# Pinning the conversion of weights and the forming of sums in a fused attention and two-MLP kernel

## The chip, the cores and the metric

The kernel runs on one core of a Trainium2 chip. The metric is the device time of one execution in microseconds (us). The core has five engines that run side by side, each working through its own instructions in order: TensorE (PE, matrix products; its weight loads are shown as PEld), VectorE (DVE), ScalarE (ACT), GpSimd (POOL) and SyncE (SP). Here POOL and SP mainly issue DMA transfers, each from its own queue.

## The reference

Linear attention feeds a first MLP, and that feeds a second one.

```python
q_s = softmax of q over the head's 64 columns          # q, k, v: 4 x 8 x 576 x 64
k_s = softmax of k over the 576 tokens
x = q_s @ (k_s.T @ v)                                  # as 2304 tokens x 512

h = x @ w_in                                           # first MLP: 512 -> 2048
g = s * relu(h) ** 2 + b
x = g @ w_out                                          # 2048 -> 512

h = x @ w_in2                                          # second MLP: 512 -> 2048
g = h * tanh(log1p(exp(min(h, 20))))                   # mish (h itself above 20 in the softplus)
out = g @ w_out2                                       # 2048 -> 512
```

The weights arrive as 64-bit floats. The kernel has to turn their bits into 32-bit floats itself.

## The kernel before, in words

**Three passes.** Most products are made of split operands. A tile t of 32-bit floats is cast on ACT to a high half (line 175), and DVE subtracts that from t to get the low half (line 172). PE then runs three fast passes: high by high, high by low, low by high (`passes`, line 178).

**First MLP.** The 2304 tokens run in five chunks of 512, 256, 512, 512 and 512. For every chunk there are 16 slots, one for each 128 columns of the hidden layer; slot n makes h of step n + 2 (`emit_h`), squares it, and adds step n into the four output banks (`emit_y`). There are 80 slots. Attention for chunk c + 1 is done in seven stages (`att1` to `att5_mm`) for four groups of two heads, spread over the slots of chunk c: for chunk 1, group hp begins in slot 2 hp + 3, with `att2` one slot later, `att3` two, `att4` three and `att5` four slots later.

**The weights of the first MLP** are made during chunk 0, in 16 pairs j, each of 128 x 1024 elements: one block of w_in (j + 1) and one of w_out (j - 1). A pair is loaded (`load_w`), then `conv_bits` takes its magnitude on ACT (line 129) and runs four DVE instructions that put the 32-bit value together in a tile t (lines 130 to 141), and `conv_split` casts and subtracts it to the halves w. Step f of the first nine h (and the first seven y) of chunk 0 uses t as it is, in slow full-precision products (lines 220 and 263); the pairs 0 to 7 are therefore split only in slots 12 to 19, the pairs 8 to 15 in slots 6 to 13. A pair j from 8 on is needed by h in slot j - 1; pair 1 and those after it are needed by chunk 1 from slot 15 + j on.

**Second MLP.** It uses a scheme of seven products (P1 to P7) for a 2 x 2 block product, instead of eight. Its inputs are sums and differences of blocks. The weights' sums are made all along the first MLP, in 32 units (`unit_sums`, `unit_split`), and stored in DRAM. Chunks are taken in pairs, (0, 2) and then (3, 4); chunk 1 comes last and in plain form. For a pair, `b_load` brings the first MLP's output back from DRAM into a tile with four spots, and `b_steps` makes the sums one product after the other, in place: `diff3`, `sum2`, `diff41`, and after each the split of one operand. The sums of pair (0, 2) are made in the last 14 slots (`put_slot`). Those of pair (3, 4) are made while pair (0, 2) is worked on: the first half goes out to DRAM (`put_dram`), the second is made later and joined with it (`put_both`). `h_unit` makes the seven products of eight such units F and adds them up into four spots of g (DVE, line 460), with mish on ACT. `y_pair` then makes the seven products of g with w_out2, splitting one spot of each g for each product (gly_P, ghy_P), and changes the spots in place between the products: in `y_pair`, too, `diff41` computes two differences in one DVE instruction of 128 x 1024. Three tiles each (tags gh and gl) hold the halves of g; `put_dram` takes its two tiles from the same three.

Weights of the second MLP come back from DRAM through a ring of tiles (`ring_load`, on the POOL queue).

**Order.** The program is traced in one order, and a planner then orders each engine's instructions by times that it works out itself. An instruction may so be put ahead of ones that were traced before it, as soon as the planner takes its inputs as ready. `pin` (`keep_in_program_order`) forbids this for one instruction: it stays behind the instruction traced just before it on the same engine. Later ones that are not pinned may still go ahead of it.

```python
        run(n, "att5", "att2", "att3", "early")
        if n < NF:
            run(n, "split", "bits")
...
        run(n, "bits", "split", "unit")
        run(n, "keep", "load")
```

These lines of the main loop fix the order inside slot n; between them lie h, the activation, the rest of attention and y.

Of the kernel before, what the change touches and what calls it, by code (L numbers as in the profile page):

```python
# [31 lines left out]
def kernel(  # L32
# [67 lines left out]

    w_raw, w_t, W = {}, {}, {}

# [21 lines left out]

    def bits(t, raw, pin=lambda ins: None):

        high, low = raw[..., 1], raw[..., 0]
        ti = t.bitcast(I32)
        pin(nc.scalar.activation(out=t, in_=high.bitcast(F32), func=AF.Abs))
# [15 lines left out]

    def conv_bits(j):
# [9 lines left out]
        raw = w_raw.pop(j)  # L156
        if j:
            bits(t, raw, pin if j > 4 else lambda ins: None)
        else:
            for i in range(2):  # L160
                bits(t[:, i], raw[:, i])

    def conv_split(j):

        home = j if j >= WHOLE else j - 1
        w = wp.tile([P, 2, 2, DM], F32R, tag=f"w{home}" if home >= 0 else "last", name=f"w{j}")
        split(w[:, :, 0], w[:, :, 1], w_t.pop(j))
        for i, (z, f) in enumerate(members(j)):
            W[z, f] = (w[:, i, 0], w[:, i, 1])
# [123 lines left out]

    def pin(ins):
        tc.keep_in_program_order(ins)

    def unit_load(e):
# [12 lines left out]
    def unit_sums(e):  # L310

        u = cv.tile([P, 8, P], F32, tag="t1", name=f"u{e}")
        u_t[e] = u
        bits(u[:, 3:7].rearrange("p b d -> p (b d)"), u_raw.pop(e), pin)
        if e + 1 < len(units):
# [30 lines left out]
    def diff3(t):  # L346
        nc.vector.tensor_tensor(out=t[:, 3], in0=t[:, 2], in1=t[:, 3], op=ALU.subtract)

    def sum2(t):
        nc.vector.tensor_tensor(out=t[:, 0], in0=t[:, 3], in1=t[:, 0], op=ALU.add)  # L350

    def diff41(t):
        nc.vector.tensor_tensor(  # L353
            out=t.rearrange("p (a b) n -> p b a n", b=2)[:, 1], in0=t[:, 1:3],
            in1=t[:, 0:1].to_broadcast([P, 2, CM]), op=ALU.subtract,
        )

    def b_steps(pair, kb, put):

        t = b_raw.pop(kb)  # L360
        if pair == 0:
            for spot in range(2):
                b = bsum[:, 2 * spot + kb:2 * spot + kb + 1]
                nc.vector.tensor_scalar(out=t[:, spot], in0=t[:, spot], scalar1=b, scalar2=None, op0=ALU.add)
        for r in Y_ORDER:
            if r == "P7":
                diff3(t)
            elif r == "P6":
                sum2(t)
            elif r == "P5":  # L370
                diff41(t)
            put(r, kb, t[:, SPOT[r]])
            yield
# [5 lines left out]
    def put_slot(r, kb, src):  # L379
        if kb == 0:  # L380
            x_op[r] = wp.tile([P, 2, 2, CM], F32R, tag=f"w{Y_ORDER.index(r)}", name=f"xo{r}")
        split(x_op[r][:, 0, kb], x_op[r][:, 1, kb], src, pin=pin)

    def put_dram(r, kb, src):
        hi, lo = g_tiles(f"b{r}_{kb}", CM)
        split(hi, lo, src)
        for i, t in enumerate((hi, lo)):
            nc.sync.dma_start(out=x_dram[r][:, i], in_=t.bitcast(F32))

    def put_both(r, kb, src):  # L390
        x_op[r] = wp.tile([P, 2, 2, CM], F32R, tag=f"w{Y_ORDER.index(r)}", name=f"xo{r}")
        pin(nc.gpsimd.dma_start(out=x_op[r][:, :, 1 - kb], in_=x_dram[r]))
        split(x_op[r][:, 0, kb], x_op[r][:, 1, kb], src)

# [47 lines left out]
    def h_unit(pair, F):  # L442
# [45 lines left out]
        ring_load()  # L488

    def y_pair(pair, more):  # L490

# [19 lines left out]
        for r in Y_ORDER:  # L511
            p[r] = ps = bank(r)
            for F in range(NU):
# [9 lines left out]
                if r == "P7" and F % 2:  # L523
                    sum2(g_all[NU // 2 + F // 2])
                if r == "P2" and F % 2:
                    diff41(g_all[F // 2])
                if r == "P6" and F % 2:
                    diff41(g_all[NU // 2 + F // 2])
                if F % 4 == 3:
# [364 lines left out]
    for j in range(NF):  # L894
        at(j - 5 if j > 4 else -3 if j < 3 else -2, "load", load_w, j)
        at(max(j - 3, -1) if j else -2, "bits", conv_bits, j)
        at(j - 2 if j >= WHOLE else NF - 4 + j, "split", conv_split, j)
    L0 = (NC - 1) * NF
# [11 lines left out]
    for kb in range(2):  # L910
        at(L0 + 2 * kb, "load", b_load, 0, kb, f"ws{kb}")
        for i in range(7):
            at(L0 + 2 + 5 * kb + i, "unit", b_next, kb)
    for s in (6, 10, 14):
        at(L0 + s, "load", ring_load)
# [33 lines left out]
    for n in range(NS):  # L949
# [7 lines left out]
        if n < NF:  # L957
            run(n, "split", "bits")
        run(n, "att4_mm")
# [14 lines left out]
        if f == NF - 1:  # L974
            y_out(c)
        run(n, "bits", "split", "unit")
        run(n, "keep", "load")
# [93 lines left out]
```

## Time and profile before

| | |
|---|---|
| time, median of 3 runs | 855.45 us (854.0 to 856.22) |
| the profiled execution: its own time, and its span | 859.47 us, 857.7 us |
| PE busy | 827.5 us, 96% of the span |
| PEld busy | 665.4 us, 78% |
| DVE busy | 615.4 us, 72% |
| ACT busy | 439.8 us, 51% |
| POOL busy | 109.1 us, 13% |
| granted TensorE clock, mean | 0.993 |

The span runs from the first to the last instruction of the profiled execution. PE's busy time is modelled and its products overlap, so the share says that PE is rarely without work, not that it runs at its best. A clock of 1.0 stands for 2.4 GHz, 0.5 for 1.2 GHz.

### The profile page before, as it was taken

How to read it: one execution, taken by the hardware profiler on the slowest of the kernel's cores; microseconds unless marked ns; L12 is line 12 of the kernel's file. 1: busy time of each engine (PE TensorE's matmuls, PEld its weight loads, DVE VectorE, ACT ScalarE, POOL GpSimd, SP SyncE). 2: the span in 40 equal slices, each digit the busy share in tenths (PEclk: the TensorE clock that was granted, in tenths of full speed). 3: DMA queues.
4: the chain of work that ended last, by engine and by line, in shares of the span. 5: the costliest groups of instructions: out<-in, count | busy, mean ns of one | idle time of the engine just before them, and what ended most of it. 6: DMA issues, size and time to landing. Idle time of an engine off the chain costs nothing.

```text
span 857.7 us, 11568 instructions
## 1 busy us (share of the span) xinstructions
PE 827.5 (96%) x4084; PEld 665.4 (78%) x4084; DVE 615.4 (72%) x1157; ACT 439.8 (51%) x787; POOL 109.1 (13%) x192
## 2 busy tenths in 40 slices
PE   4899998999999999999999999989999999999998
PEld 2444786999888888888887888778788888878897
DVE  7789897678877788877678567787764755786411
ACT  3645667557655656565565544355442333544421
POOL 4000000000000101121112211001111111112110
PEclk9999999999999999999999999999999999999999
DMA  7983422254556666467658699657678866688891
GB/s 188 313 306 113 127 77 70 68 154 131 184 188 197 212 220 217 163 207 250 206 172 255 197 362 333 192 176 237 214 247 265 235 198 204 220 295 261 259 378 59
DMA packets 90473, 179.01 MB, mean 209 GB/s; under 512 B 26928, under 2 KB 45104, under 8 KB 86832
## 3 DMA queue, kind: packets, MB, share of 16 engines
q0 software_dynamic: 30256, 112.73, 40.4%
q1 hardware_dynamic: 59072, 64.50, 24.4%
q10 hardware_dynamic: 1088, 1.05, 0.4%
q8 instruction: 32, 0.52, 0.2%
q14 instruction: 25, 0.20, 0.1%
HBM read 131.60 MB, written 46.66 MB: 208 GB/s over the span
## 4 chain that ended last, share of the span: by engine, by line
PE 57%; issue 23%; DMA 7%; DVE 6%; POOL 3%; SPq 2%; ACT 1%; POOLq 0%; DVEq 0%
PE P L182 19%; PE h L182 8%; PE y L182 8%; PE h L220 3%; PE y L263 3%; PE rh L182 3%; PE ry L182 3%; DMA xdP<-glbP 2%; POOL wdo L331 2%; DVE g L353 2%; DMA b<-yd 2%; POOL wdi L331 2%; PE P1y L182 1%; DVE gly_P L172 1%; PE P3y L182 1%
## 5 line engine op out<-in xcount | busy, mean ns | idle before, releaser
L182 PE MATMUL h<-xh,w 128*128 128x512 f32 (+1 forms) x568 | 177.2, 375 | 1.2 <-ACT xh L175 0.7
L182 PE MATMUL y<-gh,w 128*128 128x512 f32 (+1 forms) x584 | 176.2, 368 | 0.0
L182 PE MATMUL P<-xoP,rw 128*128 128x512 f32 x672 | 156.4, 390 | 3.2 <-DVE s L460 1.7
L182 PEld LDWEIGHTS P<-xoP,rw 128*128 128x128 f32 x672 | 125.4, 188 | 30.6 <-DVE s L460 3.1
L182 PEld LDWEIGHTS h<-xh,w 128*128 128x128 f32 x568 | 105.1, 192 | 19.5 <-ACT r L245 1.4
L182 PEld LDWEIGHTS y<-gh,w 128*128 128x128 f32 x584 | 106.3, 188 | 17.8
L175 ACT CAST ghy_P<-g 128x512 fp32r<-128x512 f32 x112 | 69.7, 623 | 82.5 <-DVE gly_P L172 34.6
L182 PE MATMUL y<-gl,w 128*128 128x512 f32 (+1 forms) x292 | 106.8, 367 | 0.0
L172 DVE TENSOR_TENSOR gly_P<-g,ghy_P 128x512 fp32r<-128x512 f32 x112 | 76.0, 688 | 41.4 <-ACT ghy_P L175 39.5
L182 PE MATMUL h<-xl,w 128*128 128x512 f32 (+1 forms) x284 | 105.1, 371 | 0.0
L460 DVE TENSOR_TENSOR s<-s,P 128x512 f32<-128x512 f32 x112 | 75.2, 685 | 39.9 <-PE P L182 28.9
L182 PE MATMUL P<-ghy_P,rw 128*128 128x512 f32 x224 | 87.5, 392 | 0.0
L463 ACT ACTIVATE g<-s 128x512 f32<-128x512 f32 x64 | 39.5, 631 | 76.8 <-DVE s L460 76.4
L175 ACT CAST umem<-u 128x512 fp32r<-128x512 f32 x64 | 37.3, 619 | 55.5 <-DVE u L318 54.2
L182 PEld LDWEIGHTS y<-gl,w 128*128 128x128 f32 x292 | 55.0, 188 | 9.0
L182 PEld LDWEIGHTS h<-xl,w 128*128 128x128 f32 x284 | 54.5, 192 | 8.9 <-DVE xl L172 0.3
L245 ACT ACTIVATE r<-h 128x512 f32<-128x512 f32 (+1 forms) x80 | 43.9, 552 | 31.0 <-PE h L182 20.7
L172 DVE TENSOR_TENSOR gl<-r,gh 128x512 fp32r<-128x512 f32 (+1 forms) x73 | 45.9, 629 | 18.6 <-ACT gh L175 18.2
L172 DVE TENSOR_TENSOR umem<-u,umem 128x512 fp32r<-128x512 f32 x64 | 42.3, 685 | 9.8 <-ACT umem L175 9.5
L182 PEld LDWEIGHTS P<-ghy_P,rw 128*128 128x128 f32 x224 | 42.2, 189 | 8.2
L248 ACT ACTIVATE r<-r 128x512 f32<-128x512 f32 (+1 forms) x80 | 46.8, 589 | 1.7
L182 PE MATMUL P<-gly_P,rw 128*128 128x512 f32 x112 | 45.1, 403 | 1.3 <-DVE gly_P L172 0.9
(185 smaller groups left out, 1300.7 us busy)
## 6 DMA issues: line engine op xcount, KB each, us to landing
rw<-wdo POOLq DMA_DIRECT2D x28, 1024.0 KB, 5.1
wdi<-umem POOLq DMA_DIRECT2D x32, 512.0 KB, 3.7
wdo<-umem POOLq DMA_DIRECT2D x32, 512.0 KB, 3.9
rw<-wdi POOLq DMA_DIRECT2D x16, 1024.0 KB, 7.1
rw<-wdi POOLq DMA_DIRECT2D x16, 768.0 KB, 6.6
raw<-in_moe_w_in_dram SPq DMA_DIRECT2D x16, 512.0 KB, 7.1
raw<-in_moe_w_out_dram SPq DMA_DIRECT2D x16, 512.0 KB, 9.3
ur<-in_moe_w_in_dram SPq DMA_DIRECT2D x16, 512.0 KB, 4.3
```

The lines of the kernel that those rows point to most:

```text
L172: pin(eng.tensor_tensor(out=lo, in0=src, in1=hi.bitcast(F32), op=ALU.subtract))
L175: pin(nc.scalar.copy(out=hi, in_=src))
L182: mm = nc.tensor.matmul(out=ps, lhsT=x, rhs=y, start=start, stop=stop)
L220: nc.tensor.matmul(out=h_ps[m], lhsT=wl[:, o], rhs=x_whole[kk], start=kk == 0, stop=kk == NK - 1,)
L245: op = nc.scalar.activation(out=r, in_=h_ps.pop(m), func=AF.Relu)
L248: nc.scalar.activation(out=r, in_=r, func=AF.Square)
L263: nc.tensor.matmul(out=ps, lhsT=wl[:, o], rhs=gl, start=f == 0, stop=False)
L331: nc.gpsimd.dma_start(out=to.rearrange("p b h d -> p b (h d)"), in_=u_mem[0][:, half].rearrange("p b h d -> p b (h d)"),)
L353: nc.vector.tensor_tensor(out=t.rearrange("p (a b) n -> p b a n", b=2)[:, 1], in0=t[:, 1:3], in1=t[:, 0:1].to_broadcast([P, 2, CM]), op=AL ...
L460: nc.vector.tensor_tensor(out=out, in0=a, in1=b, op=ALU.add)
L463: nc.scalar.activation(out=g[:, spot], in_=src, func=AF.Mish)
```

## The change

- The first MLP's weights are made in four events, each with its own place. `conv_size` (the magnitude on ACT) and `conv_bits` (DVE) come in slot j - 3. `conv_high` (the cast on ACT) comes at the end of slot j - 3 for the pairs from 8 on, and at the end of slot 12 + j for the first eight. `conv_low` (the subtraction on DVE) comes at the start of the slot after that, behind attention's `att5`, `att2` and `att3` of that slot. The casts and the subtractions are pinned; the magnitude stays pinned from pair 5 on. Pairs from 6 on are loaded one slot earlier, and pair 5 before the first slot.
- All sums of the second MLP's x, and their splits on both engines, are pinned (`b_steps`, `put_slot`, `put_dram`, `put_both`).
- `diff41` is gone. Each of its two differences is a DVE instruction of its own (`less0`): in `b_steps` one before P5 and one before P4, in `y_pair` at places written out in two lists (`TO3`, `TO1`) over P2, P6, P5 and P4.
- The first three ring loads move from slots 6, 10 and 14 of the last chunk to its slots 2, 9 and 14.

The arithmetic and the number of bytes moved stay the same.

```diff
-    def bits(t, raw, pin=lambda ins: None):
+    def size(t, raw, pin=lambda ins: None):
+        pin(nc.scalar.activation(out=t, in_=raw[..., 1].bitcast(F32), func=AF.Abs))
+
+    def bits(t, raw):
...
-    def conv_split(j):
+    def conv_high(j):
 
         home = j if j >= WHOLE else j - 1
         w = wp.tile([P, 2, 2, DM], F32R, tag=f"w{home}" if home >= 0 else "last", name=f"w{j}")
-        split(w[:, :, 0], w[:, :, 1], w_t.pop(j))
+        pin(nc.scalar.copy(out=w[:, :, 0], in_=w_t[j]))
+        w_new[j] = w
+
+    def conv_low(j):
+
+        w = w_new.pop(j)
+        minus(nc.vector, w[:, :, 1], w_t.pop(j), w[:, :, 0], pin)
...
-    def diff41(t):
-        nc.vector.tensor_tensor(
-            out=t.rearrange("p (a b) n -> p b a n", b=2)[:, 1], in0=t[:, 1:3],
-            in1=t[:, 0:1].to_broadcast([P, 2, CM]), op=ALU.subtract,
-        )
+    def less0(t, out, src):
+        return nc.vector.tensor_tensor(out=t[:, out], in0=t[:, src], in1=t[:, 0], op=ALU.subtract)
...
         for r in Y_ORDER:
             if r == "P7":
-                diff3(t)
+                pin(diff3(t))
             elif r == "P6":
-                sum2(t)
+                pin(sum2(t))
             elif r == "P5":
-                diff41(t)
+                pin(less0(t, 3, 2))
+            elif r == "P4":
+                pin(less0(t, 1, 1))
...
-        split(x_op[r][:, 0, kb], x_op[r][:, 1, kb], src, pin=pin)
+        split(x_op[r][:, 0, kb], x_op[r][:, 1, kb], src, pin, pin)
...
+    TO3 = tuple(("P2", F) for F in (1, 3, 4, 5, 7)) + tuple(("P6", F) for F in (1, 3, 5))
+    TO1 = tuple(("P5", F) for F in (1, 3, 5)) + tuple(("P4", F) for F in range(5))
...
-                if r == "P2" and F % 2:
-                    diff41(g_all[F // 2])
-                if r == "P6" and F % 2:
-                    diff41(g_all[NU // 2 + F // 2])
+                if (r, F) in TO3:
+                    less0(g_all[TO3.index((r, F))], 3, 2)
+                if (r, F) in TO1:
+                    less0(g_all[TO1.index((r, F))], 1, 1)
...
-        at(j - 5 if j > 4 else -3 if j < 3 else -2, "load", load_w, j)
+        at(j - 6 if j > 5 else -3 if j < 3 else -2, "load", load_w, j)
+        if j > 4:
+            at(j - 3, "early", conv_size, j, pin)
+        else:
+            at(max(j - 3, -1) if j else -2, "bits", conv_size, j)
         at(max(j - 3, -1) if j else -2, "bits", conv_bits, j)
-        at(j - 2 if j >= WHOLE else NF - 4 + j, "split", conv_split, j)
+        s = j - 3 if j >= WHOLE else NF - 4 + j
+        at(s, "keep", conv_high, j)
+        at(s + 1, "early", conv_low, j)
...
-    for s in (6, 10, 14):
+    for s in (2, 9, 14):
         at(L0 + s, "load", ring_load)
```

## Rows read from the trace of the kernel before

**Rows 1.** The page: busy time of the engines and share of the span.
```profile
PE 827.5 (96%) x4084; PEld 665.4 (78%) x4084; DVE 615.4 (72%) x1157; ACT 439.8 (51%) x787; POOL 109.1 (13%) x192
```

**Rows 2.** PE's waits: engine, line, releaser: us in total, times, longest us.
```profile
PE P1y L182 <- DVE s L460: 2.5, 1, 2.5
PE x L182 <- ACT qth L827: 2.0, 1, 2.0
...
PE P L182 <- DVE s L460: 1.7, 1, 1.7
PE P L182 <- DMA rw<-wdi: 1.5, 2, 1.2
```

**Rows 3.** Windows: stretch, its length, busy time of each engine, clock, DMA share.
```profile
142.00:148.70 6.70, 2.93 (x17) 2.01 (x15) 3.91 (x8) 5.14 (x10) 0.00 (x0) 0.86 0.33 120
148.70:153.60 4.90, 4.90 (x22) 4.85 (x23) 4.83 (x10) 4.51 (x12) 0.20 (x2) 0.50 0.23 72
456.80:458.50 1.70, 0.50 (x3) 0.11 (x2) 0.81 (x2) 1.64 (x4) 1.20 (x2) 1.00 1.07 400
...
536.40:538.70 2.30, 0.62 (x4) 0.20 (x2) 2.30 (x5) 0.04 (x1) 0.00 (x0) 1.00 0.99 301
566.60:569.40 2.80, 0.28 (x3) 0.02 (x1) 2.80 (x5) 2.23 (x5) 0.00 (x0) 1.00 0.87 322
569.40:573.50 4.10, 4.10 (x11) 3.24 (x12) 4.10 (x7) 3.22 (x6) 0.00 (x0) 0.58 0.03 12
600.00:608.00 8.00, 7.36 (x30) 5.11 (x29) 7.54 (x11) 2.86 (x5) 1.23 (x2) 1.00 0.69 231
758.00:766.00 8.00, 7.34 (x30) 5.10 (x29) 7.55 (x11) 2.85 (x5) 1.28 (x2) 1.00 0.71 234
...
597.00:608.00 11.00, 10.36 (x43) 7.52 (x42) 10.54 (x14) 4.26 (x8) 1.58 (x3) 1.00 0.70 227
608.00:619.00 11.00, 11.00 (x51) 9.07 (x50) 7.65 (x12) 4.85 (x9) 1.78 (x3) 1.00 0.64 207
```

**Rows 4.** The chain of work around 144: start, us, engine and line.
```profile
143.56 0.95 ACT w L175
...
144.53 1.23 DVE w L172
145.76 0.34 DVE qtl L172
```

**Rows 5.** DVE and POOL in order of time: start, us, what [idle before, releaser].
```profile
451.22 0.71 POOL L418 DMA_DIRECT2D rw<-wdi  x1
...
536.13 0.69 DVE L172 TENSOR_TENSOR gly_P<-g,ghy_P 128x512 fp32r<-128x512 f32 x1 [0.78 <-DMA xdP<-glbP]
...
562.53 0.69 DVE L347 TENSOR_TENSOR b<-b 128x512 f32<-128x512 f32 x1 [2.14 <-DMA b<-yd]
```

**Rows 6.** Groups by line: shapes and count, busy us, mean ns, idle before.
```profile
L172 DVE TENSOR_TENSOR w<-t,w 128x1024 fp32r<-128x1024 f32 x16 | 19.6, 1223 | 5.1 <-ACT w L175 5.1
...
L353 DVE TENSOR_TENSOR g<-g 128x1024 f32<-128x1024 f32 x16 | 19.3, 1217 | 0.1
...
L347 DVE TENSOR_TENSOR g<-g 128x512 f32<-128x512 f32 x16 | 11.0, 686 | 3.8 <-ACT g L463 3.8
```

**Rows 7.** Chunk 0: two of attention's DVE steps, in order of time.
```profile
99.91 0.42 DVE L764 TENSOR_TENSOR qn<-q,qs 128x256 f32<-128x256 f32 x1
...
137.47 0.42 DVE L764 TENSOR_TENSOR qn<-q,qs 128x256 f32<-128x256 f32 x1
```

**Rows 8.** The chain of work: the first h products of slots 8 and 12.
```profile
95.36 1.13 PE h L182 x5
...
120.57 1.81 PE h L182 x8
```

**Rows 9.** DMA issues: queue, count, KB each, median us from issue to landing.
```profile
yd<-ys SPq DMA_DIRECT2D x16, 256.0 KB, 2.8
...
xdP<-glbP SPq DMA_DIRECT2D x7, 256.0 KB, 9.5
```

More of the change, by code (lines that the diff above doesn't have):

```diff
@@ L98, in segments, with pin @@
         return found
-    w_raw, w_t, W = {}, {}, {}
+    def pin(ins):
+        tc.keep_in_program_order(ins)
+    w_raw, w_t, w_new, W = {}, {}, {}, {}
     def members(j):
@@ L123, in load_w @@
         w_raw[j] = raw.rearrange("p z (n w) -> p z n w", w=2)
-    def bits(t, raw, pin=lambda ins: None):
+    def size(t, raw, pin=lambda ins: None):
+        pin(nc.scalar.activation(out=t, in_=raw[..., 1].bitcast(F32), func=AF.Abs))
+    def bits(t, raw):
         high, low = raw[..., 1], raw[..., 0]
         ti = t.bitcast(I32)
-        pin(nc.scalar.activation(out=t, in_=high.bitcast(F32), func=AF.Abs))
         nc.vector.tensor_scalar(
@@ L144, in bits, with conv_size @@
         )
-    def conv_bits(j):
+    def conv_size(j, pin=lambda ins: None):
         if j < WHOLE:
@@ L155, in conv_bits @@
             W[z, f] = (None, t[:, i])
-        raw = w_raw.pop(j)
         if j:
-            bits(t, raw, pin if j > 4 else lambda ins: None)
+            size(t, w_raw[j], pin)
+    def conv_bits(j):
+        t, raw = w_t[j], w_raw.pop(j)
+        if j:
+            bits(t, raw)
         else:
             for i in range(2):
+                size(t[:, i], raw[:, i])
                 bits(t[:, i], raw[:, i])
-    def conv_split(j):
+    def conv_high(j):
         home = j if j >= WHOLE else j - 1
         w = wp.tile([P, 2, 2, DM], F32R, tag=f"w{home}" if home >= 0 else "last", name=f"w{j}")
-        split(w[:, :, 0], w[:, :, 1], w_t.pop(j))
+        pin(nc.scalar.copy(out=w[:, :, 0], in_=w_t[j]))
[3 more added lines that the diff above has]
+        minus(nc.vector, w[:, :, 1], w_t.pop(j), w[:, :, 0], pin)
         for i, (z, f) in enumerate(members(j)):
@@ L292 @@
     u_mem, u_raw, u_t = [], {}, {}
-    def pin(ins):
-        tc.keep_in_program_order(ins)
     def unit_load(e):
@@ L313, in unit_sums @@
         u_t[e] = u
-        bits(u[:, 3:7].rearrange("p b d -> p (b d)"), u_raw.pop(e), pin)
+        raw = u_raw.pop(e)
+        size(u[:, 3:7].rearrange("p b d -> p (b d)"), raw, pin)
+        bits(u[:, 3:7].rearrange("p b d -> p (b d)"), raw)
         if e + 1 < len(units):
@@ L346, in diff3 @@
     def diff3(t):
-        nc.vector.tensor_tensor(out=t[:, 3], in0=t[:, 2], in1=t[:, 3], op=ALU.subtract)
+        return nc.vector.tensor_tensor(out=t[:, 3], in0=t[:, 2], in1=t[:, 3], op=ALU.subtract)
     def sum2(t):
-        nc.vector.tensor_tensor(out=t[:, 0], in0=t[:, 3], in1=t[:, 0], op=ALU.add)
-    def diff41(t):
-        nc.vector.tensor_tensor(
-            out=t.rearrange("p (a b) n -> p b a n", b=2)[:, 1], in0=t[:, 1:3],
-            in1=t[:, 0:1].to_broadcast([P, 2, CM]), op=ALU.subtract,
-        )
+        return nc.vector.tensor_tensor(out=t[:, 0], in0=t[:, 3], in1=t[:, 0], op=ALU.add)
+    def less0(t, out, src):
+        return nc.vector.tensor_tensor(out=t[:, out], in0=t[:, src], in1=t[:, 0], op=ALU.subtract)
     def b_steps(pair, kb, put):
@@ L363, in b_steps @@
                 b = bsum[:, 2 * spot + kb:2 * spot + kb + 1]
-                nc.vector.tensor_scalar(out=t[:, spot], in0=t[:, spot], scalar1=b, scalar2=None, op0=ALU.add)
+                pin(nc.vector.tensor_scalar(out=t[:, spot], in0=t[:, spot], scalar1=b, scalar2=None, op0=ALU.add))
         for r in Y_ORDER:
             if r == "P7":
-                diff3(t)
+                pin(diff3(t))
             elif r == "P6":
-                sum2(t)
+                pin(sum2(t))
             elif r == "P5":
-                diff41(t)
+                pin(less0(t, 3, 2))
+            elif r == "P4":
+                pin(less0(t, 1, 1))
             put(r, kb, t[:, SPOT[r]])
@@ L381, in put_slot @@
             x_op[r] = wp.tile([P, 2, 2, CM], F32R, tag=f"w{Y_ORDER.index(r)}", name=f"xo{r}")
-        split(x_op[r][:, 0, kb], x_op[r][:, 1, kb], src, pin=pin)
+        split(x_op[r][:, 0, kb], x_op[r][:, 1, kb], src, pin, pin)
     def put_dram(r, kb, src):
         hi, lo = g_tiles(f"b{r}_{kb}", CM)
-        split(hi, lo, src)
+        split(hi, lo, src, pin, pin)
         for i, t in enumerate((hi, lo)):
@@ L392, in put_both @@
         pin(nc.gpsimd.dma_start(out=x_op[r][:, :, 1 - kb], in_=x_dram[r]))
-        split(x_op[r][:, 0, kb], x_op[r][:, 1, kb], src)
+        split(x_op[r][:, 0, kb], x_op[r][:, 1, kb], src, pin, pin)
     ring, ring_at = [], [0, 0]
@@ L957 @@
         if n < NF:
-            run(n, "split", "bits")
+            run(n, "bits")
         run(n, "att4_mm")
@@ L975 @@
             y_out(c)
-        run(n, "bits", "split", "unit")
+        run(n, "unit")
         run(n, "keep", "load")
```

## The prediction

> **What bounds the kernel now.** I read the page first: PE is busy for 96% of the span, DVE for 72% [rows 1]. So the end is set by PE, and a change that removes no product can only win where PE stands still or runs at half clock, and can only lose by adding such places. The next view is PE's own list of waits [rows 2]. It is short. Setting aside the start, which the change leaves as it is, the long ones are for DVE's sums of the second MLP's products (line 460: 2.5 and 1.7 us), for a high half in attention (2.0 us) and for a ring load (1.2 us at its longest). The third view, windows cut around these places [rows 3], prices them. PE's idle time is the length of a window less its busy time:
>
> - 142.0 to 148.7 (chunk 0 turns into chunk 1): 6.70 - 2.93 = 3.8 us idle. The clock falls behind it. At 0.86 over 6.7 us, 28% or 1.9 us of the window run at 1.2 GHz instead of 2.4, then 4.9 us at 0.50. Half of that time is lost, 3.4 us. Together 7.2 us.
> - 456.8 to 458.5: 1.2 us, the ring load.
> - 536.4 to 538.7: 1.7 us, behind line 460.
> - 566.6 to 569.4: 2.5 us, behind line 460, and then a clock of 0.58 over 4.1 us, so 3.4 us at 1.2 GHz, 1.7 us lost. Together 4.2 us.
> - 600 to 608 and 758 to 766: 0.6 and 0.7 us, in the products with w_out2 of either pair. DVE is busy there for 10.54 of 11 us, against 7.65 in the next 11 us.
>
> That is 15.6 us in six places; the half clock came only behind the two longest stops. All six lie where the change works. Sums go against the profiled execution, 859.47 us; I take them off the median of 855.45 us unscaled, since both are the same program 4 us apart.
>
> **The first MLP's weights.** Removed: nothing. The 16 casts and 16 subtractions stay, 1.22 us of DVE each [rows 6]. What changes is that they can't float any more. At 142 us PE waits for the x of attention's last group, and the chain of work to that x runs through a weight's cast (0.95 us) and a weight's subtraction (1.23 us), and only then comes attention's own subtraction qtl [rows 4]. The half being made there belongs to pair 5 (counted along the 16), which the code places in slot 17; PE is at the end of slot 15. With the pins, pair 5's cast is at the end of slot 17, behind the activation traced there, so those two steps leave the chain: 0.95 + 1.23 = 2.2 us. What remains of the 3.8 us is 1.6 us, shorter than the 1.7 us at 536.4, behind which the next window shown still has a clock of 1.00 [rows 3]. So I also count the 3.4 us of half clock as won: 5.6 us. Bounds: nothing (other work fills the chain) and all 7.2 us. I take 5.6, the steps seen in the chain.
>
> The price is that a low half now stands behind attention. In slots 7, 9 and 11 `conv_low` is pinned behind `att3`, whose last DVE step is qn, and qn needs the buffer that PE's x of the group before must first release. For group 1 (groups counted from 0) qn ended at 99.91 + 0.42 = 100.33 us; a low half behind it ends at 101.6. But slot 8's h, which reads it, started at 95.36 [rows 7, 8]: 6.2 us late. For group 3 it is 137.89 + 1.23 = 139.1 against 120.57: 18.5 us late. Below, the price is nothing: qn was itself held up by the floating halves and bits in front of it, PE can take attention's small products ahead of h, and DVE's four steps of `bits`, not pinned, can fill the wait. I charge one qn and one low half once, 0.4 + 1.2 = 1.65 us, near the lower end, since a pair's nominal slot still lies a whole slot ahead of its use. Queued behind a waiting low half are the next pair's bits and then the activation's low halves; two steps of h ahead cover those.
>
> The magnitude was pinned before, from pair 5 on, and moves within its slot. The loads one slot earlier concern SyncE's queue alone, and by the code's order their tiles are free then: nothing on the path. In chunk 1 the splits of pairs 3 to 7 no longer run ahead, so some 5 x 1.2 = 6 us of DVE work moves behind 150 us, two slots ahead of its use: no charge, covered by DVE's idle time there; if that cover is gone, each costs PE at most its 1.2 us.
>
> **The ring loads.** The first load was issued at 451.22 [rows 5], pinned on POOL's queue behind a weight store of its slot, and PE waited for it 1.2 us. Four slots earlier takes it past the stores of two or three units on that queue; its tile ("last") is free since the last chunk began. It then lands well ahead of PE: 1.2 us won, lower bound nothing. The second and third loads shift by one slot and none, and no wait of PE names them.
>
> **The pinned sums.** At 562.53 DVE had stood for 2.14 us at `diff3` of the second half of pair (3, 4), waiting for b to land [rows 5]. This step is needed only for the pair after. Behind it in DVE's order stood the sums of line 460 that PE waited for until 569.4. Pinned, the step is behind the P7 products' low halves, tens of us after the load. The stop and its half clock go: 4.2 us, lower bound nothing (see the rivals). At 536.13 DVE stood 0.78 us, for the second time in a row, at a low half of g for `y_pair`, whose tile was still being written out by `put_dram` [rows 5]; the sums that PE wanted came after it. With the x sums pinned in units 2 to 6 the three tiles are taken later, and such a low half can't be put ahead of all of them any more: 1.7 us, lower bound nothing. The seven splits that move into `y_pair` add a step of some 0.69 us to each product of about 11 us, where DVE has 3.3 us free outside P2 [rows 3].
>
> **The differences apart.** One 128 x 1024 step took 1.217 us, two of 128 x 512 take 2 x 0.686 = 1.372 us [rows 6]: 0.155 us more, 20 times, 3.1 us of DVE work in all. In exchange eight double steps that all fell into P2 become 16 single ones over four products. The saturated stretch loses three of its eight double steps' worth, 8 x 1.217 - 5 x 0.686 = 6.3 us of DVE time, and three other products get 2.1 to 3.4 us, which about fills the 3.3 us that DVE had free from 608 to 619. The two stops go: 0.64 + 0.66 = 1.3 us, lower bound nothing.
>
> The Trainium skill (VectorE: DVE Perf Modes, section on the TRN2 errata) speaks against this edit: each DVE instruction on SBUF pays a fixed latency, a large tile once and small ones each time. The rows agree with it by the 0.155 us per split; by that rule, the edit costs DVE time and wins none.
>
> **The sum.** 5.6 + 1.2 + 4.2 + 1.7 + 1.3 = 14.0 us won, 1.65 us paid: 12.35 us. 855.45 - 12.35 = 843.1 us (847.1 for an execution such as the profiled one).
>
> **The rivals.**
>
> - *Only the second MLP wins* (0.16): attention's last group is late in its own right (1.6 of the 3.8 us stay in the sum above as they are, and other work may fill the rest), and the turn of chunks keeps its 7.2 us. 855.45 - 8.4 = 847.0 us.
> - *The stores take the place of the waits removed* (0.10): `put_dram`'s last two tiles now leave at the end of unit 6, and the first low halves of `y_pair` need those tiles. A store took 9.5 us to land here, against 2.8 us for the same size elsewhere [rows 9]; a unit has 42 products of 512 columns, which at 11.00 / 49 = 0.224 us each [rows 3] make 9.4 us of PE. At the first figure PE waits at P1, at the second not. Then the 4.2 and 1.7 us come back: 843.1 + 5.9 = 849.0 us. For it: DVE already waited for these stores. Against it: the stores are now spread, which thins the traffic that made them slow.
> - *DVE becomes the bound in the products with w_out2* (0.06): all 3.1 us of the splitting lie on the path: 846.2 us. For it: in pair (0, 2) the 3.4 us and a moved split make 4.1 us against 3.3 us free. Against it: that holds for one product of seven. This is where the rule of the Trainium skill named above would lead.
> - *No change* (0.12): the planner puts other steps of as much work into the same places: 855 us.
> - *Slower: the low halves behind attention* (0.16): in slots 7 to 13 every pair waits for a step of attention that runs late by more than a slot. The price lies between 6.2 and 18.5 us from the rows above; halfway it is 12.4 us, the turn of chunks wins nothing, and 855.45 - 8.4 + 12.4 = 859.5 us. It decides from 8.4 + 2.6 = 11 us of lateness on. For it: the rows as they stand. Against it: they describe an attention that had the halves in front of it.
>
> **How the numbers follow.** The forecast has 0.40; its own range is 837 to 849 us. About 0.3%, 2.6 us, is what a measurement of this kernel can tell from no change. Faster (below 852.9): 0.40 + 0.16 + 0.10 + 0.06 = 0.72. Same: 0.12. Slower: 0.16. The range reaches down to all 15.6 us won without a price, 839.8, less 2.6 for small stops that I haven't priced: 837. Up it takes in no change with its 2.6 us: 858. Left out is the slower case, and little else.
>
> **What would show it.** Right: after about 142 us the clock stays at 1.00 and no weight's cast or subtraction lies between attention's qth and qtl; PE's list of waits loses the ring load of 1.2 us and the two for line 460; `diff3` of b shows no idle time for a DMA; DVE's busy share is even over P2 to P4 and PE has no idle time there. Wrong: PE waits for "DVE w L172" between 90 and 135 us, or for a low half of g at the first product with w_out2, with xdP as what DVE waits for.

## The result, and the profile after

| | before | after |
|---|---|---|
| time, median | 855.37 us (853.11 to 857.78, 16 runs) | 862.04 us (857.89 to 868.7, 16 runs) |
| profiled execution: own time, span | 859.47 us, 857.7 us | 868.7 us, 866.9 us |
| granted TensorE clock, mean | 0.993 | 0.985 |

The ratio is 1.0083, 95% interval [1.0065, 1.0101]: the change makes the kernel 0.8% slower. That is 18.9 us above the forecast of 843.1 us and 4 us above the range.

The profiled execution of after is the slowest of its 16. Their mean clock runs from 0.985 (span 866.9 us) to 0.996 (span 856.1 us). By an estimate, half clock costs (1 - clock) x span: 13.0 us in the first, 3.4 us in the second. The spans differ by 10.8 us, and some 9 of these are half clock (a second execution of 856.1 us shows 0.995). So the profile shows the stops at their dearest. The profile of before is a dear one too: 859.47 us lies above all 16 times of that kernel, so the prices that the prediction read from it may be high. The table below shows that for 520 to 600 us.

The page of after, busy time of the engines (as [rows 1]):

```profile
PE 831.3 (96%) x4084; PEld 669.3 (77%) x4084; DVE 619.7 (71%) x1177; ACT 441.2 (51%) x787; POOL 108.5 (13%) x192
```

The products are the same 4084; what has grown is the time between them and the time at half clock. PE's waits in after (as [rows 2]: line waiting, releaser, us in total, times, longest):

```profile
PE P L199 <- DMA rw<-wdi: 3.8, 1, 3.8
PE P L199 <- DVE gly_P L189: 3.7, 2, 2.9
PE h L199 <- ACT r L262: 3.1, 1, 3.1
PE h L199 <- ACT w L178: 2.5, 3, 1.5
...
PE x L199 <- DVE qtl L189: 1.4, 2, 1.2
```

The waits of before for line 460, for qth and for the first ring load [rows 2] are gone from the list. Four others stand there. The windows of after (as [rows 3]: length, busy time of each engine, clock, DMA share) put a price on the stops:

```profile
120.00:140.00 20.00, 17.09 (x98) 13.72 (x96) 19.10 (x33) 12.68 (x25) 0.10 (x1) 1.00 0.22 59
140.00:153.00 13.00, 12.15 (x64) 10.53 (x65) 8.90 (x16) 9.75 (x17) 0.30 (x3) 0.87 0.30 95
462.00:465.00 3.00, 1.29 (x3) 1.10 (x4) 1.90 (x3) 2.94 (x7) 1.25 (x2) 0.63 0.00 0
465.00:475.00 10.00, 10.00 (x36) 7.96 (x36) 8.13 (x16) 6.59 (x12) 1.84 (x4) 0.77 0.51 168
500.00:507.00 7.00, 3.18 (x15) 2.34 (x14) 4.37 (x7) 4.46 (x6) 1.40 (x2) 1.00 0.97 271
507.00:512.00 5.00, 5.00 (x17) 3.96 (x16) 0.77 (x2) 0.58 (x1) 0.00 (x0) 0.66 1.12 397
574.00:581.00 7.00, 3.30 (x12) 1.78 (x10) 2.46 (x5) 1.77 (x3) 0.53 (x1) 0.84 0.80 298
581.00:588.00 7.00, 7.00 (x22) 5.35 (x21) 6.21 (x11) 4.20 (x7) 0.53 (x1) 0.67 0.01 5
600.00:608.00 8.00, 8.00 (x37) 6.60 (x37) 7.79 (x14) 4.10 (x8) 1.22 (x2) 1.00 0.69 243
758.00:766.00 8.00, 8.00 (x37) 6.63 (x36) 7.42 (x13) 3.66 (x6) 1.51 (x3) 1.00 0.75 256
```

The first two windows hold the turn of chunks. From 140 to 153 us PE is idle for 0.9 us and loses 0.13 x 13 = 1.7 us to half clock, together 2.6 us in place of 7.2 before; but from 120 to 140 us it now stands for 2.9 us, where before it didn't stand. The last two windows are those in which PE stood for 0.6 and 0.7 us before [rows 3]; now it doesn't stand there at all. (By then the stages come some 11 to 13 us later in after: the product P2 of the first pair begins at 603.7 us, against 591.1. From 600 to 660 us and from 740 to 800 us nothing is lost.) The three long new stops are near 464, 506 and 580 us, each with half clock behind it.

**Stages of all kernels.** To compare traces I cut each into windows of 20 us from its start, and take as lost the length less PE's busy time, plus (1 - clock) x 20. A moment in which PE stands still at half clock counts twice, and the rounded clock leaves 0.1 us for each window. Every line is one profiled execution; the kernels are those of the next section.

| us lost in | 80-160 | 160-320 | 440-480 | 480-520 | 520-600 | 600-620, 740-780 | 80-840 |
|---|---|---|---|---|---|---|---|
| before | 7.2 | 0.2 | 1.5 | 0.3 | 6.0 | 1.3 | 16.5 |
| after | 6.5 | 3.3 | 6.5 | 5.6 | 7.1 | 0.0 | 29.0 |
| weights_only | 6.2 | 1.5 | 0.4 | 0.0 | 3.2 | 0.9 | 12.2 |
| weights_low_free | 5.0 | 0.2 | 0.0 | 0.4 | 2.9 | 0.7 | 9.3 |
| pins02_only | 7.0 | 0.2 | 2.2 | 5.5 | 2.4 | 1.4 | 18.7 |
| pins02_low_free | 7.6 | 0.2 | 4.1 | 5.3 | 2.9 | 1.4 | 21.5 |
| pins02_early | 5.5 | 0.2 | 5.6 | 1.7 | 4.0 | 1.3 | 18.4 |
| pins02_ahead | 7.2 | 0.2 | 0.0 | 3.9 | 2.3 | 1.3 | 14.9 |
| pins34_only | 5.2 | 0.2 | 1.0 | 0.5 | 3.4 | 1.4 | 11.7 |
| pins34_own_tiles | 7.4 | 0.2 | 1.1 | 0.0 | 1.1 | 1.3 | 11.2 |
| apart_only | 6.6 | 0.2 | 0.4 | 1.3 | 2.5 | 0.0 | 11.0 |
| apart_both | 7.0 | 0.2 | 1.1 | 0.8 | 1.0 | 0.0 | 10.3 |
| all_but_02 | 8.0 | 1.5 | 0.0 | 0.2 | 0.8 | 0.0 | 10.4 |
| after_ahead | 6.6 | 3.3 | 0.0 | 1.7 | 6.2 | 0.0 | 17.8 |
| best | 5.0 | 0.2 | 1.0 | 0.0 | 0.0 | 0.0 | 6.2 |

Before to after: 440 to 520 us gives 10.3 of the 12.5 us; 160 to 320 us gives 3.1. The measure overstates: the spans of the two differ by 9.2 us, the medians by 6.7. The stretch 520 to 600 is read with care: the two kernels with the weights' events alone and the four called pins02 have the code of before for the work there, and lost 2.3 to 4.0 us in place of 6.0, so single executions differ there by their stops and by whether half clock follows one.

### The profile page after: what moved, and what is told of

Same layout as the page of the kernel before. It is cut to its first block, busy times and chain, and to the rows that moved or that the text cites. A ratio compares the mean times of both kernels' runs of the same rounds, so it can differ in the third digit from the quotient of the medians.

```text
span 866.9 us, 11575 instructions
## 1 busy us (share of the span) xinstructions
PE 831.3 (96%) x4084; PEld 669.3 (77%) x4084; DVE 619.7 (71%) x1177; ACT 441.2 (51%) x787; POOL 108.5 (13%) x192
## 4 chain that ended last, share of the span: by engine, by line
PE 78%; DVE 7%; DMA 6%; issue 4%; ACT 3%; SPq 1%; POOL 1%; DVEq 0%; POOLq 0%; ACTq 0%
PE P L199 24%; PE h L199 15%; PE y L199 15%; PE h L237 3%; PE y L280 3%; PE rh L199 3%; PE ry L199 3%; DMA xdP<-glbP 2%; DMA ur<-in_moe_w_out_dram 2%; PE P1y L199 2%; DMA kb<-in_k_dram 1%; PE P3y L199 1%; PE P5y L199 1%; PE P7y L199 1%; PE P4y L199 1%
## 5 line engine op out<-in xcount | busy, mean ns | idle before, releaser
L199 PEld LDWEIGHTS y<-gh,w 128*128 128x128 f32 x584 | 107.4, 190 | 18.6 <-ACT w L178 0.4
```

The lines of the kernel that those rows point to most:

```text
L199: mm = nc.tensor.matmul(out=ps, lhsT=x, rhs=y, start=start, stop=stop)
```

## The experiments

Every kernel was timed in five rounds beside the kernel before on the same chip; that kernel's median was 854.95 us beside the first set, 855.59, 855.19 and 854.78 us beside the others. `free`, or a `pin` left out, means that the planner places the instruction.

### First set: one part each

**weights_only**: the four events and the loads that go with them; all of the second MLP and the ring loads as before.

```diff
+        s = j - 3 if j >= WHOLE else NF - 4 + j
+        at(s, "keep", conv_high, j)
+        at(s + 1, "early", conv_low, j)
```

> The kernel before with one part of the change: the first MLP's weights in four events, with their loads. The theory of the prediction (the splits leave attention's way, one low half late): 1.65 - 5.6 = -4.0 us, so 851.4 us. The theory from the trace after (the halves pinned behind attention stop PE at several places from 106 to 142 us, and ACT waits there for the DVE bits of the weights): between +0 and +6 us, some 858 us, with waits of PE for ACT w and DVE qtl in that stretch.

Measured: 856.32 us, ratio 1.0017 [1.0003, 1.0032]. Nothing is won. The wait for qth of 2.0 us [rows 2] is gone, and 140 to 160 us lost 1.7 us in place of 7.2. But 100 to 140 us lost 4.5, where before lost nothing; PE now waits three times for a weight's cast:

```profile
PE h L199 <- ACT w L178: 2.5, 3, 1.5
...
PE x L199 <- DVE qtl L189: 1.3, 2, 1.1
```

**pins02_only**: the x sums of the chunks (0, 2) and their low halves pinned, with the differences there apart.

(`hold` is `pin` for these chunks and `free` for the others.)

```diff
-                diff41(t)
+                if hold is pin:
+                    pin(less0(t, 3, 2))
+                else:
+                    diff41(t)
...
-        split(x_op[r][:, 0, kb], x_op[r][:, 1, kb], src, pin=pin)
+        split(x_op[r][:, 0, kb], x_op[r][:, 1, kb], src, pin, pin)
```

> The kernel before with one part of the change: the x sums of chunks (0, 2) pinned and their differences apart, the ring loads where they were. The prediction charged nothing here: 855 us. The theory from the trace after (ACT's pinned casts of these sums wait for DVE's sums, the pinned activation of the first MLP stands behind them, and a ring tile comes free late): a wait of PE for ACT r near 464 us and one for a ring load near 506 us, together 3 to 10 us with the clock that falls behind them, some 860 us.

Measured: 861.93 us, ratio 1.0077 [1.006, 1.0094]. This part alone has nearly the whole loss. PE's long wait is for a ring tile (4.9 us in two, longest 3.9). That tile's load was issued at 492.24 us, after POOL had waited 3.62 us for the last low half of these x. (POOL waited for that low half before as well, 4.30 us, but the load left at 487.99 us.)

**pins34_only**: the same pins on the pairs (1, 0) and (1, 1) alone, `put_dram` and `put_both`.

```diff
-        split(hi, lo, src)
+        split(hi, lo, src, pin, pin)
```

> The kernel before with one part of the change: the x sums of chunks (3, 4) pinned and their differences apart. The prediction: the stops near 538 and 569 us go, 1.7 + 4.2 = -5.9 us, 849.5 us. The theory from the trace after (the stores of the sums leave later, and the first low halves for w_out2 wait for their tiles): these stops go, but one of 3 to 4 us with half clock takes their place at the first product with w_out2, so 854 to 857 us.

Measured: 854.43 us, ratio 0.9996 [0.9985, 1.0008]. No difference. The stop near 537 us is not there (520 to 560 us lost nothing), and PE waits for gly_P, 4.1 us in seven waits. The four kernels pins02_*, which don't pin this pair, lost nothing in that stretch either.

**apart_only**: in `y_pair` alone, the double differences as two instructions each at the places of `TO3` and `TO1`.

```diff
-                if r == "P2" and F % 2:
-                    diff41(g_all[F // 2])
+                if (r, F) in TO3:
+                    less0(g_all[TO3.index((r, F))], 3, 2)
```

> The kernel before with one part of the change: the differences of the products with w_out2 apart and spread over four products. The prediction and the trace after agree on -1.3 us, 854.1 us, with no idle time of PE in the products P2 to P4 of either pair. If DVE's extra 0.155 us for each were on the path: up to +2.5 us, 858 us.

Measured: 851.59 us, ratio 0.9964 [0.9949, 0.998]. The stops at 600 to 608 and 758 to 766 us are gone:

```profile
600.00:608.00 8.00, 8.00 (x37) 6.64 (x36) 4.27 (x7) 3.58 (x7) 0.56 (x1) 1.00 0.75 266
758.00:766.00 8.00, 8.00 (x37) 6.63 (x36) 5.20 (x9) 3.59 (x7) 1.75 (x3) 1.00 0.92 287
```

The four ratios add up to 1.4 + 6.6 - 0.3 - 3.1 = 4.6 us, against 7.1 us for the whole. The intervals leave room for that difference, and the move of the ring loads is in none of the four. The traces show more: the stop at 464 us is in after and not in pins02_only, so the parts are not independent.

### Second set: what is it about each part?

**all_but_02**: the whole change, with the x of the chunks (0, 2) as before.

```diff
-            b_gen[kb] = b_steps(0, kb, put_slot)
+            b_gen[kb] = b_steps(0, kb, put_slot, free)
```

> The whole change, except that the x sums of the chunks (0, 2) of the second MLP, their differences, their high halves on ScalarE and their low halves are placed by the scheduler as in the kernel before. Theory (the pinned sums of (0, 2) are the loss, by a late ring tile at 500 us and by the stop at 464 us): 6 to 8 us come back, the time is 854 to 856 us, and neither stop is in the trace. Rival (the first MLP's weights in four events are the loss): 860 to 862 us, with both stops gone and the stops of the first 240 us left.

Measured: 852.32 us, ratio 0.9969 [0.9946, 0.9992]. Some 9.7 us come back; 440 to 520 us lost 0.2. The loss comes with these pins and the differences apart that go with them.

**pins02_early**: pins02_only, with the second half's sums one slot earlier.

```diff
-            at(L0 + 2 + 5 * kb + i, "unit", b_next, kb)
+            at(L0 + 2 + 4 * kb + i, "unit", b_next, kb)
```

> The pinned sums of the chunks (0, 2) alone, with the second half's sums one slot earlier for every slot (its steps stand at slots 6 to 13 in place of 7 to 14). Theory (what costs 7 us is that the last step frees the ring tile 4 us late, so that its load lands at 499.5 us and TensorE then runs at half clock): the load lands before 496 us, the stop at 499.7 us is gone, the time is 854 to 857 us. Rival (the pins make ScalarE and VectorE wait for each other and TensorE behind them): the time stays at 860 to 862 us, with the stop elsewhere.

Measured: 860.14 us, ratio 1.0059 [1.0042, 1.0076]. The theory fell: the late ring tile isn't the whole cause. 480 to 520 us lost 1.7 us in place of 5.5, yet the kernel is hardly faster. PE's wait for the tile shrank only to 1.7 us, since the load was issued 1.85 us earlier and took 8.5 us to land (before, 7.0). And 440 to 480 us lost 5.6 in place of 2.2: a new stop stands at 460 us, where PE's h waits for relu:

```profile
PE h L185 <- ACT r L248: 3.8, 2, 3.0
PE P L185 <- DMA rw<-wdi: 1.7, 1, 1.7
```

**apart_both**: apart_only, and of the pins only those of `put_both`.

```diff
+            steps_b = b_steps(1, 1, put_both, pin)
```

> The double differences apart, as in the run apart_only (851.6 us), and of the pins only those of the last x sums, (1, 1), that go both to SBUF and to DRAM. Theory (the wait of 1.7 us at 536 us and the wait at 566 us both stand before sums that these pins bring forward; each was followed by half clock): 4 us come off, 847 to 849 us. Rival (the wait for the stores moves to another tile, as in pins34_only, and gives the gain back): 851 to 852 us, with a wait of PE for gly_P in 560 to 580 us.

Measured: 849.62 us, ratio 0.9931 [0.9911, 0.9951]. 520 to 600 us lost 1.0, and no wait for gly_P is listed there. The pins on the last sums are worth about 2.8 us on top of apart_only (0.9964 to 0.9931); the intervals don't tell this from the expected 4 us.

**weights_low_free**: weights_only, with the low halves not pinned.

```diff
-        minus(nc.vector, w[:, :, 1], w_t.pop(j), w[:, :, 0], pin)
+        minus(nc.vector, w[:, :, 1], w_t.pop(j), w[:, :, 0])
```

> The first MLP's weights in four events alone, as in the run weights_only (856.3 us), with the low halves of the weights placed by the scheduler and the other three events as in the change. Theory (the low halves ahead of attention's operands are what hands the gain back): 852 to 853 us, and the waits of TensorE for km and q in 160 to 220 us are shorter. Rival (the casts and magnitudes on ScalarE, pinned early, are what others wait for): 856 to 857 us, with the waits of h for ScalarE's w left.

Measured: 853.16 us, ratio 0.9967 [0.9951, 0.9984]: faster than before. Against weights_only, 80 to 160 us lost 1.2 us less and 160 to 320 us 1.3 us less. The waits of h for a weight's cast are still there (2.1 us in two, against 2.5 in three), and 100 to 140 us still lost 4.3. Whether the casts' pins or their earlier place do that, no run isolates; the cast at 125.01 us had itself waited 0.67 us for DVE's bits.

### Third set: which pin of the chunks (0, 2), and what is worth keeping

**pins02_low_free**: pins02_only, with the 14 low halves not pinned.

```diff
-        split(x_op[r][:, 0, kb], x_op[r][:, 1, kb], src, pin, pin)
+        split(x_op[r][:, 0, kb], x_op[r][:, 1, kb], src, pin)
```

> The pinned sums of the chunks (0, 2) alone, as in pins02_only (861.9 us), but with the 14 low halves on VectorE placed by the scheduler; the sums and differences on VectorE stay pinned, and the high halves on ScalarE are pinned as in both kernels. Theory (the sums' and differences' fixed place behind a unit's operations is the loss: the pinned casts on ScalarE wait for them, and relu and the next ring tile wait for the casts): the time stays at 859 to 862 us and the casts' waits of 4.1 us are left. Rival (each pinned low half makes VectorE wait 0.69 us for its cast, 14 times, and that ends the x sums late): 854 to 857 us, with the ring tile's load landing before 497 us.

Measured: 861.92 us, ratio 1.007 [1.0058, 1.0083]. The low halves have no part in it that the intervals show. The sums do, and the group of ACT's 14 casts that these x need shows how (420 to 505 us; under a group's durations stands for whom its engine sat idle before it, in us and times). The kernel before:

```profile
L175 ACT CAST xoP<-b x14: 603/616/619, 424.7 to 486.3; 128x512 fp32r<-128x512 f32 x14
its engine sat idle before it (us, times) until:
who waited for it (us, times):
```

pins02_low_free:

```profile
L178 ACT CAST xoP<-b x14: 604/620/624, 423.2 to 491.0; 128x512 fp32r<-128x512 f32 x14
its engine sat idle before it (us, times) until:
  DVE b L353: 7.9, 4
  DVE b L350: 5.5, 2
  DVE b L347: 2.9, 2
  DVE b L370: 2.3, 2
```

Before, no cast waited for its sum. With the sums pinned ACT stands idle for 18.6 us in ten of them, and the last cast begins 4.7 us later. (In pins02_only and in after it is 19.1 us, by the same four sorts of sum.)

**pins34_own_tiles**: pins34_only, with the halves that `put_dram` stores in two other tiles.

```diff
-        hi, lo = g_tiles(f"b{r}_{kb}", CM)
+        own = cv.tile([P, 2, CM], F32R, tag=f"t{Y_ORDER.index(r) % 2}", name=f"bo{r}_{kb}")
+        hi, lo = own[:, 0], own[:, 1]
```

> The pinned sums of the pairs (1, 0) and (1, 1) alone, as in pins34_only (854.4 us), with the halves that go to DRAM alone put into two tiles of the kernel's pool that the step's work leaves free there, in place of the two gh and gl tiles that the units' g operands take next. Theory (the operands of the first units wait for the stores that still read those two tiles; that wait took the place of the one removed): PE's waits of 4.1 us for gly_P go and the time is 849 to 851 us. Rival (the pinned sums crowd VectorE itself, so that the g operands come late whatever tile they take): 854 to 855 us, with those waits left.

Measured: 852.44 us, ratio 0.9968 [0.9955, 0.9981], between what the two expected and 2 us below pins34_only. In pins34_only DVE's list of waits had this line, and here it has none for a store:

```profile
DVE gly_P L175 <- DMA xdP<-glbP: 3.4, 2, 2.0
```

520 to 600 us lost 1.1 in place of 3.4. PE still waits 2.2 us for gly_P (4.1 in pins34_only), so about half of that wait went with the stores. What holds the rest, no run isolates.

**best** and **best_own**: weights_low_free and apart_both in one kernel, ring loads as before; best_own has the pins of (1, 0) and the own tiles as well.

```diff
-            steps_b = b_steps(1, 1, put_both)
+            steps_b = b_steps(1, 1, put_both, pin)
...
+        minus(nc.vector, w[:, :, 1], w_t.pop(j), w[:, :, 0])
```

> What the parts say is worth keeping: the weights in four events with the low halves free (weights_low_free, 2.4 us faster than before), the double differences apart and the pins on the last x sums, (1, 1), alone (apart_both, 6.0 us). No pins on the chunks (0, 2) nor on (1, 0), ring loads where they were. Theory (the stages are independent): 855.5 - 2.4 - 6.0, 846 to 848 us. Rival (a stop that one part removes comes back with the other, as the one at 464 us did with all parts of the change): 850 us or more.

> As best, and also the pins on (1, 0) with the halves for DRAM in tiles of their own, as in pins34_own_tiles. Theory (the wait for the stores was the only harm of these pins): at or below best, 845 to 848 us. Rival (pins on (1, 0) do harm of their own on VectorE): 850 to 852 us.

Measured: best 846.7 us, ratio 0.9904 [0.9888, 0.992]; best_own 846.67 us, ratio 0.9893 [0.988, 0.9905]. Both beat the kernel before by 1% and after by 1.8%. Here the parts do add up (0.9967 x 0.9931 = 0.9898). What is left in best between 440 and 600 us is the stop near 456 us, the one for the first ring load, which was not moved here; 5.0 of its 6.2 us lie from 80 to 160 us. The windows from 440 us on:

```profile
440.00:480.00 40.00, 39.03 (x172) 32.01 (x172) 33.96 (x69) 25.88 (x46) 8.00 (x11) 1.00 0.69 224
480.00:520.00 40.00, 40.00 (x178) 32.94 (x177) 24.84 (x38) 17.79 (x29) 7.29 (x11) 1.00 0.96 318
560.00:600.00 40.00, 40.00 (x178) 32.95 (x177) 36.19 (x60) 22.37 (x37) 6.27 (x11) 1.00 0.70 228
```

### Fourth set: the pins, or the place to which they hold?

**pins02_ahead** and **after_ahead**: pins02_only and the whole change, every pin kept, with each sum traced behind the split of the operand before it instead of ahead of its own (`own(r)` makes the pinned sum or difference that r needs; the pairs (1, 0) and (1, 1) keep their order).

```diff
-        for r in Y_ORDER:
+        def own(r):
...
+        ahead = pair == 0
+        for r, after in zip(Y_ORDER, Y_ORDER[1:] + ("",)):
+            if not ahead:
+                own(r)
             put(r, kb, t[:, SPOT[r]])
+            if ahead:
+                own(after)
             yield
```

> The pinned sums of the chunks (0, 2) alone, as in pins02_only (861.9 us), with every pin kept, and each operand's sum or difference written behind the split of the operand before it, so one slot of some 7 us ahead of its own cast, in place of just ahead of it. Theory (a pinned sum is held until 0.7 us before its cast, ScalarE's next cast in its fixed order waits for it, and what stands behind is late): the casts' waits are gone, the last low half ends before 490 us, the ring tile lands before 497 us, the time is 854 to 857 us. Rival (it is the pins as such, in whatever place: VectorE can no longer take other work first): 860 to 862 us.

> The whole change with the same single edit: the sums and differences of the chunks (0, 2) stay pinned, one slot ahead of their casts. Theory: what all_but_02 gave (852.3 us), 851 to 855 us, with the stops at 464 us and at 500 to 507 us gone. Rival (the pins as such): 859 to 862 us.

Measured: pins02_ahead 854.77 us, ratio 0.9998 [0.9986, 1.0011]; after_ahead 852.15 us, ratio 0.9962 [0.9945, 0.9979]. The same pins in another place cost nothing, and the whole change with this one edit is faster than before. ACT's casts in pins02_ahead:

```profile
L178 ACT CAST xoP<-b x14: 603/616/621, 423.1 to 484.2; 128x512 fp32r<-128x512 f32 x14
its engine sat idle before it (us, times) until:
  DVE b L370: 5.4, 2
```

Eight of the ten waits are gone; the two left are for the first sum of each half (line 370), which has no slot ahead. They grew from 2.3 to 5.4 us, and PE didn't wait behind them: 440 to 480 us lost nothing. For P5's operand of the first half the sum and the cast now stand 5.2 us apart (DVE, then ACT):

```profile
439.98 0.69 DVE L353 TENSOR_TENSOR b<-b 128x512 f32<-128x512 f32 x1
```

```profile
445.20 0.62 ACT L178 CAST xoP<-b 128x512 fp32r<-128x512 f32 x1
```

One thing was not as expected: in pins02_ahead 480 to 520 us still lost 3.9, with a wait of 2.1 us near 504 us for a later ring tile, whose load took 11.2 us to land. In after_ahead the stop at 464 us is gone and 480 to 520 us lost 1.7, but 520 to 600 us lost 6.2, with PE waiting 2.7 us for gly_P.

## Why the prediction was wrong

**The step that failed** is the paragraph on the pinned sums. It priced the sums of the pair (3, 4) and left those of the chunks (0, 2) without a word, so at nothing. They cost 6.6 us alone (pins02_only) and 9.7 us in the whole change (862.04 to 852.32). The mechanism, in after, around 464 us (start, us, engine and line, what, idle before and releaser):

```profile
459.01 0.69 DVE L369 TENSOR_TENSOR b<-b 128x512 f32<-128x512 f32 x1
...
459.73 0.62 ACT L192 CAST xoP<-b 128x512 fp32r<-128x512 f32 x1 [4.09 <-DVE b L369]
...
461.51 0.62 ACT L192 CAST xoP<-b 128x512 fp32r<-128x512 f32 x1 [1.16 <-DVE b L377]
462.03 1.13 ACT L192 CAST umem<-u 128x512 fp32r<-128x512 f32 x2
...
463.07 0.59 ACT L262 ACTIVATE r<-h 128x512 f32<-128x512 f32 x1
...
463.71 0.79 PE L199 MATMUL h<-xh,w 128*128 128x512 f32 x1 [3.09 <-ACT r L262]
```

A sum is traced as the last work of its slot. Pinned, it stays behind the DVE work of the unit in that slot, and ends 0.03 us before its cast begins. The casts on ACT were pinned in the kernel before as well, so ACT can't pass them: it stands for 4.09 and 1.16 us. Behind them in ACT's order come the unit's casts and then relu, which must empty the bank that PE's next h needs. Not pinned, they ran well ahead: the double difference for P5 and P4 of the first half began at 435.62 us, and P5's cast, the fifth of that half, at 447.92. In the kernel before (DVE, then ACT):

```profile
435.62 1.22 DVE L353 TENSOR_TENSOR b<-b 128x1024 f32<-128x1024 f32 x1
```

```profile
447.92 0.62 ACT L175 CAST xoP<-b 128x512 fp32r<-128x512 f32 x1
```

That is a lead of 12.3 us, and no cast there ever waited. The Trainium skill (PSUM — Partial Sum Buffer, Engine vs sequencer instructions) calls ScalarE's and VectorE's queues strictly first in, first out; the trace agrees, since relu began only behind the late casts, at 463.07 us.

The same lateness runs on to the end of the stage: the last low half ends later, and the ring tile that held these sums comes free later. In after POOL waits 3.61 us for it:

```profile
498.58 1.42 POOL L433 DMA_DIRECT2D rw<-wdi  x2 [3.61 <-DVE xoP L189]
```

This load landed at 505.79 us, and PE waited 3.8 us for it. That the place is the cause and not the pin is shown by pins02_ahead and after_ahead. Why the stop falls at 464 us in the whole change, at 500 us in pins02_only and at 460 us in pins02_early is not settled; the drift of the parts against each other by a few us would do it, but no run isolates that.

The other steps:

- **The weights** (5.6 us won, 1.65 paid): the gain came, and the price was mis-sized. In weights_only 140 to 160 us lost 5.5 us less than before. But 100 to 140 us lost 4.5 more and 160 to 320 us 1.3 more, so 5.8 us were paid in place of 1.65, and the kernel is 1.4 us slower by its ratio. Pinned low halves are a part of this: without their pins 1.0017 became 0.9967, some 4.3 us by the ratios, though the traces show only 1.2 of these before 160 us and 1.3 from there to 320. Most of the price from 100 to 140 us stayed without them (4.3 of 4.5 us), and there PE's long waits were for the casts on ACT (2.5 us in after), not for low halves (0.2), which the prediction had named as the sign of being wrong. DVE was also fuller there: 19.1 of the 20 us from 120 to 140 in after, 16.5 before. So the rival that feared the low halves had a part of the mechanism, at 12.4 us a price some three times too high.
- **The first ring load** (1.2): the wait is gone in after, all_but_02 and after_ahead, which move the load, and 440 to 460 us of after is without a stop. But it is gone in weights_low_free and pins02_ahead too, which don't move it, and no run tries this edit by itself. So its worth is not shown.
- **The stop near 537 us** (1.7): 520 to 560 us lost nothing in after and in pins34_only, but nothing in the four kernels pins02_* either, which leave this pair unpinned. That the pins removed it is not shown.
- **The stop near 567 us** (4.2): `diff3`'s wait for b is gone as said, but the rival with the stores came at this place, to which I gave 0.10, and with it the second sign of being wrong. The 4.2 us were also those of a dear execution: with the same code there, the six kernels named under the table lost 2.3 to 4.0 us from 520 to 600 us in all. DVE in after:

```profile
571.01 0.69 DVE L189 TENSOR_TENSOR gly_P<-g,ghy_P 128x512 fp32r<-128x512 f32 x1 [1.35 <-DMA xdP<-glbP]
...
579.33 0.69 DVE L189 TENSOR_TENSOR gly_P<-g,ghy_P 128x512 fp32r<-128x512 f32 x1 [3.14 <-DMA xdP<-glbP]
```

  My argument against it, that the stores are spread and so faster, held only in part: they take 6.1 us in the median against 9.5 [rows 9], but the last one, issued at 571.0 us, took 8.3, and DVE's low half began when it landed.
- **The differences apart** (1.3): right in place, and too small. The two stops are gone and the kernel gains 3.1 us. The rule of the Trainium skill (VectorE: DVE Perf Modes, section on the TRN2 errata) that I set against this edit is right on cost here (the 16 splits of apart_only cost 1.8 us of DVE's busy time; in after all of DVE's work grew by 4.3 us, of which 3.1 were expected). What I drew from it, that the edit wins no time, did not come. Where the other 1.8 of the 3.1 us won come from is not shown; the planner moved other work as well.
- **The half clock** was counted as won where a stop went. It came back behind each new long stop, as the windows at 465, 507 and 581 us show. At the turn of chunks it was counted as won because a stop of 1.6 us would be left, shorter than the one of 1.7 us with a clock of 1.00 behind it. In after PE stands for 1.7 us from 138 to 142 us, and the window from 140 to 153 us has a clock of 0.87 all the same, so the length of a stop did not decide.
- **A reading**: the rival with the stores took 49 products in 11.00 us; the window named for it in [rows 3] has 51, which makes a unit 9.1 us of PE in place of 9.4. Nothing turns on it.

## What to carry to other kernels

A pin doesn't only forbid early work, it fixes the work at the place where it was traced: before pinning a producer, look how far ahead of its consumer it ran, and trace it that far ahead. If the consumer sits in the fixed order of another engine, that engine's whole queue inherits the wait. And when a change has several parts, time each: here one part of four cost 9.7 us, and hid that another was worth having as it stood and two more in part (the weights with free low halves, the pins on the last sums).

## What was unexpected in the hardware

The time of one and the same kernel varied together with TensorE's granted clock: in after from 0.985 to 0.996 of 2.4 GHz, and by the estimate above some 9 of the 10.8 us between the longest and the shortest of its spans are time at 1.2 GHz. So a stop can cost more than its own length: in after PE stood still for 3.8 us between 500 and 507 us, and the five us behind had a clock of 0.66, another 1.7 us.

Length alone doesn't tell when that happens. In weights_only and in all_but_02 PE stands for 1.7 us near 142 us; behind it the clock stays at 1.00 in the one and falls in the other, for 0.09 x 20 = 1.8 us:

```profile
140.00:160.00 20.00, 18.34 (x123) 16.68 (x122) 15.78 (x28) 17.18 (x32) 0.58 (x5) 1.00 0.24 82
```

```profile
140.00:160.00 20.00, 18.33 (x114) 16.54 (x112) 14.35 (x26) 16.10 (x29) 0.48 (x5) 0.91 0.24 82
```

What decides, these runs don't show. A kernel with several such stops is harder to time, and a single profile of it need not be a typical one.
